# Batch-wide decays, a re-ordered start and half-column last stores in a linear-attention plus gated-MLP kernel

## Chip, cores and metric

One core of one Trainium2 chip. The metric is device time in microseconds (us) of one execution. Each execution has a state: "slow" ones lie over 1.5% above the fastest of the same kernel, and are left out of every comparison of times. A ratio below is the mean time of one kernel's fast runs over that of the other's of the same rounds, so it is not quite the ratio of the medians that are quoted beside it. The kernel before was timed again in each call, and the calls of the experiments ran on different chips of the same kind.

## The reference

Per batch (4) and head (8), blocks of 64 of 768 tokens; scores decay with the distance of tokens, a state carries what lies before the block. The result goes through a gated MLP whose gate is mixed over the tokens.

```python
Dmask = np.where(rel >= 0, lam ** rel, 0.0)
for b in range(nb):
    intra = (qb @ kb.T * Dmask) @ vb
    inter = (qb * lam ** (pos + 1)) @ kv_state
    out[b] = intra + inter
    kv_state = lam ** block * kv_state + (kb * lam ** (block - 1 - pos)).T @ vb
# x = heads side by side, (4, 768, 512)
h = relu(x @ w_in); u, v = halves of h
v_n = layernorm(v); v_s = w_spatial @ v_n + b_spatial      # over tokens
out = (u * v_s) @ w_out
```

## The kernel before

It works in 12 steps of 256 tokens, three to a batch. TensorE, GpSimd (POOL) and the sync engine (SP) run in the order of the program text; VectorE (DVE) and ScalarE (ACT) are ordered by the framework's scheduler. GpSimd prepares what was loaded (`ck` multiplies k by its decays into the tile `kd`, `cq` and `cv` cast q and v to bf16 as `qc` and `vc`), and in the same in-order queue issues the loads of the weights (`win`, `wsp`, `wout`). The load of v of step 1 is split: one half by SP, one by ScalarE.

```python
lam_bc = const.tile([P, H], FP32)
nc.scalar.dma_start(out=lam_bc, in_=lam...)
load_step(0)                               # k (two DMAs) and q on nc.sync; v too where n >= 2
load_v(0, nc.scalar, (0,))
load_step(1)
load_v(1, nc.sync, (1,))                   # cut: the tile is made here
for n in range(2, 4):
    load_step(n)
# ... cut ...
lq = const.tile([P, NG, T2], BF16)
for g in range(NG):
    last = nc.scalar.activation(out=lq[:, g, :], in_=qpos, func=AF.Exp, scale=logl[:, g:g + 1])
with tc.issue_after(last.ins):
    load_v(0, nc.scalar, (1,))
    load_v(1, nc.scalar, (0,))
# ... cut: kv_step ...
        sd = att.tile([P, NG, D], FP32, tag="sd", name=f"sd_{n}_{c}")
        nc.vector.tensor_tensor(out=sd, in0=prev, in1=lb, op=ALU.mult)
        nc.vector.tensor_tensor(out=s_sb[:, c], in0=sd, in1=pkv[:, c], op=ALU.add)
# ... cut: the order of the start (T: transposes, A: scores, K: states, O: outputs of attention) ...
run("""
    mask ck:0 cq:0 ck:1 cv:0 win:1 cq:1 cv:1 c:2 win:0 wsp wout c:3 lk:4 lk:5 lk:6
    T:0 K:0 A:0 T:1 O:0 K:1 A:1 pv:0:0 O:1 T:2 K:2 pv:0:1 A:2 pu:0:0 O:2
    c:4 pu:0:1 wt:0 pv:0:2 wt:2 pu:0:2 wt:4
    ...
""")
```

`wt:0` holds the first transposes of the spatial weight (tile `pwt`): nothing of batch 0 beyond them can run before that weight has landed. Its first matmul is the milestone in what follows.

Of the kernel before, what the change touches and what calls it, by code (L numbers as in the profile page):

```python
# [9 lines left out]
FP32 = mybir.dt.float32  # L10
BF16 = mybir.dt.bfloat16
I32 = mybir.dt.int32
# [6 lines left out]
def kernel(  # L19
# [13 lines left out]
    P = 128  # L33
# [57 lines left out]
    load_step(0)  # L91
    load_v(0, nc.scalar, (0,))
    load_step(1)
    st[1]["v_in"] = fin.tile([P, H, 2, D], FP32, tag="v_in", name="v_in_1")
    load_v(1, nc.sync, (1,))
    for n in range(2, 4):
        load_step(n)


    krev_i = const.tile([P, 1], I32)  # L100
    nc.gpsimd.iota(krev_i, pattern=[[0, 1]], base=P - 1, channel_multiplier=-1)

    qpos_i = const.tile([P, 2, 2, D], I32)
    nc.gpsimd.iota(qpos_i, pattern=[[1, 2], [0, 2], [2, D]], base=1, channel_multiplier=0)

# [4 lines left out]

    krev = const.tile([P, 1], FP32)
    nc.vector.tensor_copy(out=krev, in_=krev_i)
# [13 lines left out]
    for hh in range(2):  # L126
        rows = slice(hh * D, (hh + 1) * D)
        nc.vector.tensor_copy(out=logl[rows, :], in_=loglam[rows, hh::2])
    ldec = const.tile([P, H], FP32)
    nc.scalar.activation(out=ldec, in_=loglam, func=AF.Exp, scale=krev[:, 0:1])  # L130
    lm128 = const.tile([P, H], FP32)
    nc.scalar.activation(out=lm128, in_=loglam, func=AF.Exp, scale=-float(P))
    lq = const.tile([P, NG, T2], BF16)
    for g in range(NG):
        last = nc.scalar.activation(out=lq[:, g, :], in_=qpos, func=AF.Exp,
                                    scale=logl[:, g:g + 1])
    with tc.issue_after(last.ins):
        load_v(0, nc.scalar, (1,))
        load_v(1, nc.scalar, (0,))
    l128 = const.tile([P, NG], FP32)  # L140
    nc.scalar.activation(out=l128, in_=logl, func=AF.Exp, scale=float(P))
    sq_t = const.tile([P, 1], FP32)
    with tc.issue_after(last.ins):
        nc.scalar.activation(out=sq_t, in_=eps_t, func=AF.Sqrt)
    amask = const.tile([P, 2, 2, 2, P], FP32)

    def make_amask():
        for i in range(2):
            nc.vector.tensor_tensor(
                out=amask[:, i], in0=causal.unsqueeze(1).unsqueeze(1).broadcast_to((P, 2, 2, P)),  # L150
                in1=lm128[:, 4 * i:4 * i + 4].rearrange("p (g h) -> p h g", h=2).unsqueeze(3)
                .broadcast_to((P, 2, 2, P)), op=ALU.mult)

    win_sb = wpool.tile([P, NCH, DFF], BF16)
    wout_sb = wpool.tile([P, NCH, DM], BF16)
# [19 lines left out]
    def cast_step(n, parts=("k", "q", "v")):  # L175
        s = st[n]
        for part in parts:
            cast_part(s, n, part)

    def cast_part(s, n, part):  # L180
        if part == "k":
            kd = s["kd"] = att.tile([P, 2, H, D], BF16, tag="kd", bufs=4, name=f"kd_{n}")
            nc.gpsimd.tensor_tensor(out=kd.rearrange("p c h d -> p h c d"), in0=s["k_in"],  # L183
                                    in1=ldec.unsqueeze(2).unsqueeze(3).broadcast_to((P, H, 2, D)),
                                    op=ALU.mult)
        elif part == "q":
            qc = s["qc"] = att.tile([P, 2, H, D], BF16, tag="qc", bufs=4, name=f"qc_{n}")
            nc.gpsimd.tensor_copy(out=qc.rearrange("p m h d -> p h m d"), in_=s["q_in"])  # L188
        else:
            vc = s["vc"] = att.tile([P, H, 2, D], BF16, tag="vc", bufs=4, name=f"vc_{n}")  # L190
            nc.gpsimd.tensor_copy(out=vc, in_=s["v_in"])  # L191

    def trans_step(n):
        kd, qc = st[n]["kd"], st[n]["qc"]
        pt = two_banks([P, 2, NG, T2], f"pt_{n}", BF16)
        for j, src in ((0, kd), (1, qc)):
            for g in range(NG):
                for c in range(2):
# [4 lines left out]
        kT = att.tile([P, NG, T2], BF16, tag="kT", name=f"kT_{n}")  # L203
        nc.scalar.activation(out=kT, in_=pt[:, 0], func=AF.Copy)  # L204
        qT = att.tile([P, NG, 2, 2, D], BF16, tag="qT", name=f"qT_{n}")
        nc.vector.tensor_tensor(out=qT.rearrange("p g m a d -> p g (m a d)"), in0=pt[:, 1],  # L206
                                in1=lq, op=ALU.mult)
        st[n]["qT"], st[n]["kT"] = qT, kT
# [4 lines left out]
    def scores_step(n):  # L213
# [5 lines left out]
        for i in range(2):  # L219
            pam = two_banks([P, 2, 2, 2, P], f"pam_{n}_{i}")  # L220
            for g2 in range(2):
# [8 lines left out]
                in0=pam.rearrange("p h g c x -> p (h g) c x"),  # L230
                in1=amask[:, i].rearrange("p h g x -> p (h g) x").unsqueeze(2)
                .broadcast_to((P, 4, 2, P)), op=ALU.mult)

    def kv_step(n):
# [11 lines left out]
        s_sb = att.tile([P, 2, NG, D], BF16, tag="s_sb", name=f"s_{n}")  # L246
        lb = l128.unsqueeze(2).broadcast_to((P, NG, D))
        for c in range(nb):
            prev = s_sb[:, 0] if c == 1 else (st[n - 1]["s"][:, 1] if r > 0 else None)
            if prev is None:  # L250
                nc.vector.tensor_copy(out=s_sb[:, c], in_=pkv[:, c])
            else:
                sd = att.tile([P, NG, D], FP32, tag="sd", name=f"sd_{n}_{c}")
                nc.vector.tensor_tensor(out=sd, in0=prev, in1=lb, op=ALU.mult)  # L254
                nc.vector.tensor_tensor(out=s_sb[:, c], in0=sd, in1=pkv[:, c], op=ALU.add)
        st[n]["s"] = s_sb
# [81 lines left out]
    def pvs(b, f):  # L338
        m = gm[b]
        ps = two_banks([P, 2, 512], f"pvs_{b}_{f}")  # L340
        for i in range(2):
            cols = slice(i * HW_, (i + 1) * HW_)
            for s in range(NBLK):
# [7 lines left out]
                                op=ALU.mult)  # L351

    def po(b, r):
        gT = gm[b]["gT"]
        ps = two_banks([P, 2, DM], f"po_{b}_{r}")
# [5 lines left out]
        o_sb = ostg.tile([P, 2, DM], FP32, tag="o_sb", name=f"o_{b}_{r}")  # L361
        if (b, r) == (B - 1, NR - 1):
            dst = out[b, r * T2:(r + 1) * T2, :].rearrange("(j p) f -> p j f", p=P)
            half = slice(0, DM // 2), slice(DM // 2, DM)
            nc.scalar.activation(out=o_sb[:, 0], in_=ps[:, 0], func=AF.Copy)
            nc.sync.dma_start(out=dst[:, 0], in_=o_sb[:, 0])
            nc.vector.tensor_copy(out=o_sb[:, 1, half[0]], in_=ps[:, 1, half[0]])
            nc.scalar.activation(out=o_sb[:, 1, half[1]], in_=ps[:, 1, half[1]], func=AF.Copy)
            nc.sync.dma_start(out=dst[:, 1, half[0]], in_=o_sb[:, 1, half[0]])
            nc.scalar.dma_start(out=dst[:, 1, half[1]], in_=o_sb[:, 1, half[1]])  # L370
            return
        nc.scalar.activation(out=o_sb, in_=ps, func=AF.Copy)  # L372
# [3 lines left out]
    def wt_piece(s):  # L376
        ps = two_banks([P, 2, 1024], f"pwt_{s}", BF16)
        for j in range(2):
# [9 lines left out]
            "po": po, "wt": wt_piece, "win": load_win, "wsp": load_wsp, "wout": load_wout,  # L388
            "mask": make_amask, **{"c" + x: lambda n, x=x: cast_step(n, (x,)) for x in "kqv"}}

    def run(text):
# [5 lines left out]
    run("""  # L397
        mask ck:0 cq:0 ck:1 cv:0 win:1 cq:1 cv:1 c:2 win:0 wsp wout c:3 lk:4 lk:5 lk:6
        T:0 K:0 A:0 T:1 O:0 K:1 A:1 pv:0:0 O:1 T:2 K:2 pv:0:1 A:2 pu:0:0 O:2
        c:4 pu:0:1 wt:0 pv:0:2 wt:2 pu:0:2 wt:4  # L400
        c:5 lk:7 pvs:0:0 pvs:0:1 T:3 pvs:0:2 A:3 K:3 c:6 pvs:0:3 T:4 po:0:0
# [56 lines left out]
```

## Time and profile before

| | before |
|---|---|
| median, 4 runs | 177.33 us (176.49 to 177.79); the prediction had 3 of them, 177.02 |
| span of the profiled execution (a slow one) | 180.9 us |
| spatial weight issued, first `pwt` matmul | 28.39, 42.63 us |
| VectorE busy | 106.0 us |

The prediction below reads this profile stretch by stretch.

### The profile page before, as it was taken

To read this page: it belongs to the slowest core of one execution; us is meant where nothing else is said; L and a number is where in the kernel's file an instruction comes from. 1 tells how busy PE (TensorE), PEld (TensorE's weight loads), DVE (VectorE), ACT (ScalarE), POOL (GpSimd) and SP (SyncE) were. 2 spreads that over 40 slices of the span, in tenths; PEclk is the share of its full clock that TensorE was granted. 3 is DMA by queue.
4 is the path that set the end of the run, shared out by engine and by line. 5 is a ranking of instruction groups with operands and counts; after the bars stand their busy time and mean duration, and the time that the engine had idled before them with its cause. 6 is when DMAs were issued, how large, how long until landed. Compare 5 with 4: busy or idle time off the path is not lost.

```text
span 180.9 us, 3629 instructions
## 1 busy us (share of the span) xinstructions
PE 145.4 (80%) x1528; PEld 95.2 (53%) x1540; DVE 106.0 (59%) x182; ACT 77.3 (43%) x88; POOL 53.2 (29%) x50
## 2 busy tenths in 40 slices
PE   0041699399869999997955999999999999999890
PEld 0031566176636665676742655567866645776430
DVE  0712988921652889579998447179994713834400
ACT  2940057237911045677450014756822257660051
POOL 2439639400555566207556702000000000000000
PEclk9999999969987999999997899999999999999997
DMA  3999999999999999999899900630000026000036
GB/s 79 266 224 239 212 243 224 194 202 200 239 226 218 253 216 270 321 263 196 220 238 224 236 5 0 235 116 4 0 4 0 0 104 248 0 0 5 0 126 222
DMA packets 68497, 28.36 MB, mean 157 GB/s; under 512 B 50560, under 2 KB 65536, under 8 KB 68480
## 3 DMA queue, kind: packets, MB, share of 16 engines
q1 hardware_dynamic: 62560, 24.25, 58.2%
q0 software_dynamic: 2512, 2.95, 9.4%
q10 hardware_dynamic: 3408, 0.92, 2.7%
q8 instruction: 12, 0.20, 0.5%
q14 instruction: 5, 0.04, 0.1%
HBM read 24.78 MB, written 6.29 MB: 172 GB/s over the span
## 4 chain that ended last, share of the span: by engine, by line
PE 53%; DVE 17%; DMA 12%; SPq 9%; ACT 3%; issue 1%; POOL 1%; ACTq 0%; POOLq 0%
PE pvs L344 17%; PE po L359 10%; DMA wsp_raw<-in_moe_w_spatial_dram 8%; PE pv L313 8%; PE pu L334 7%; SPq L78 5%; DVE a L228 5%; DMA v_in<-in_v_dram 5%; DVE vn L325 4%; PE pvs L346 3%; PE pt L199 3%; DVE gT L348 2%; SPq L80 2%; DVE st L319 2%; SPq L69 2%; DVE sd L254 2%
## 5 line engine op out<-in xcount | busy, mean ns | idle before, releaser
L344 PE MATMUL pvs<-wt_sb,vn 128*128 128x384 bf16 x192 | 39.8, 343 | 5.2 <-DVE vn L325 5.1
L228 DVE TENSOR_TENSOR a<-pam,amask 128x1024 bf16<-128x1024 f32 x24 | 28.5, 1211 | 3.4 <-PE pam L225 3.4
L183 POOL TENSOR_TENSOR kd<-k_in,ldec 128x1024 bf16<-128x1024 f32 x12 | 23.0, 1917 | 23.2 <-DMA k_in<-in_k_dram 16.2
L344 PEld LDWEIGHTS <-vn 128*128 128x128 bf16 x192 | 19.4, 103 | 19.6 <-DVE vn L325 6.3
L204 ACT ACTIVATE kT<-pt 128x1024 bf16<-128x1024 bf16 x12 | 12.2, 1021 | 38.9 <-PE pt L199 38.9
L348 DVE TENSOR_TENSOR gT<-pvs,uT 128x768 bf16<-128x768 f32 x16 | 15.3, 957 | 19.6 <-PE pvs L346 19.6
L334 PE MATMUL pu<-xT,win_sb 128*128 128x256 bf16 x192 | 24.0, 284 | 2.9 <-DMA win_sb<-in_moe_w_in_dram 2.9
L313 PE MATMUL pv<-win_sb,xT 128*128 128x512 bf16 x89 | 22.0, 380 | 1.9 <-ACT xT L288 1.6
L359 PE MATMUL po<-wout_sb,gT 128*128 128x512 bf16 x91 | 21.7, 379 | 1.4 <-DVE a L228 0.7
L319 DVE BATCH_NORM_STATS2 st<-vh 128x6 f32<-128x512 bf16 x24 | 15.4, 682 | 12.5 <-ACT vh L316 12.3
L334 PEld LDWEIGHTS <-win_sb 128*128 128x128 bf16 x192 | 19.2, 102 | 6.6 <-DMA win_sb<-in_moe_w_in_dram 3.0
L288 ACT ACTIVATE xT<-pat 128x1024 bf16<-128x1024 f32 x12 | 15.8, 1320 | 15.6 <-PE pat L285 15.4
L191 POOL CAST vc<-v_in 128x1024 bf16<-128x1024 f32 x12 | 12.8, 1066 | 28.1 <-DMA v_in<-in_v_dram 20.9
L372 ACT ACTIVATE o<-po 128x1024 f32<-128x1024 f32 x11 | 11.3, 1025 | 18.3 <-PE po L359 18.3
L336 ACT ACTIVATE uT<-pu 128x1024 bf16<-128x1024 f32 x12 | 12.2, 1021 | 10.1 <-PE pu L334 10.1
L316 ACT ACTIVATE vh<-pv 128x1024 bf16<-128x1024 f32 x12 | 12.2, 1021 | 8.2 <-PE pv L313 8.1
L199 PE MATMUL pt<-ident,kd 128*128 128x128 bf16 x96 | 8.2, 234 | 9.1 <-POOL kd L183 9.1
L359 PEld LDWEIGHTS <-gT 128*128 128x128 bf16 x96 | 9.1, 98 | 11.7 <-DVE gT L348 1.3
L313 PEld LDWEIGHTS <-xT 128*128 128x128 bf16 x96 | 8.9, 98 | 11.3 <-ACT xT L288 2.0
L188 POOL CAST qc<-q_in 128x1024 bf16<-128x1024 f32 x12 | 12.9, 1076 | 5.9 <-DMA q_in<-in_q_dram 5.7
L206 DVE TENSOR_TENSOR qT<-pt,lq 128x1024 bf16<-128x1024 bf16 x12 | 8.2, 684 | 10.7 <-ACT kT L204 10.7
L325 DVE TENSOR_SCALAR vn<-vh,mv,rstd 128x512 bf16<-128x512 bf16 x24 | 14.1, 629 | 0.3
(54 smaller groups left out, 142.0 us busy)
## 6 DMA issues: line engine op xcount, KB each, us to landing
k_in<-in_k_dram SPq DMA_DIRECT2D x24, 256.0 KB, 5.3
q_in<-in_q_dram SPq DMA_DIRECT2D x12, 512.0 KB, 6.7
out_dram<-o SPq DMA_DIRECT2D x11, 512.0 KB, 3.1
v_in<-in_v_dram SPq DMA_DIRECT2D x21, 256.0 KB, 6.5
wsp_raw<-in_moe_w_spatial_dram POOLq DMA_DIRECT2D x1, 1152.0 KB, 14.2
win_sb<-in_moe_w_in_dram POOLq DMA_DIRECT2D x2, 512.0 KB, 8.2
v_in<-in_v_dram ACTq DMA_DIRECT2D x3, 256.0 KB, 6.3
wout_sb<-in_moe_w_out_dram POOLq DMA_DIRECT2D x1, 512.0 KB, 17.4
```

The costliest lines, as they stand in the source:

```text
L183: nc.gpsimd.tensor_tensor(out=kd.rearrange("p c h d -> p h c d"), in0=s["k_in"], in1=ldec.unsqueeze(2).unsqueeze(3).broadcast_to((P, H, 2, ...
L188: nc.gpsimd.tensor_copy(out=qc.rearrange("p m h d -> p h m d"), in_=s["q_in"])
L199: nc.tensor.transpose(out=pt[:, j, g, c * P:(c + 1) * P], in_=src[:, c, 2 * g:2 * g + 2, :].rearrange("p h d -> p (h d)"), identity=ident)
L228: nc.vector.tensor_tensor(out=a_sb[:, i].rearrange("p h g c x -> p (h g) c x"), in0=pam.rearrange("p h g c x -> p (h g) c x"), in1=amask[: ...
L288: nc.scalar.activation(out=xT[b][:, r].rearrange("p g (c d m) -> p (g c) m d", c=2, m=2), in_=po.rearrange("p g c (m d) -> p (g c) m d", m ...
L313: nc.tensor.matmul(out=ps[:, j], lhsT=x[:, r, c, j * P:(j + 1) * P], rhs=win_sb[:, c, DH:DFF], start=(c == 0), stop=(c == NCH - 1))
L319: nc.vector.bn_stats(out=m["st6"][:, t, :], in_=vh[:, t, :])
L325: nc.vector.tensor_scalar(out=m["vn"][:, t, :], in0=vh[:, t, :], scalar1=mv[:, t, 0:1], scalar2=rstd[:, t:t + 1], op0=ALU.subtract, op1=AL ...
L334: nc.tensor.matmul(out=ps[:, f], lhsT=win_sb[:, c, f * P:(f + 1) * P], rhs=x[:, r, c, :], start=(c == 0), stop=(c == NCH - 1))
L344: nc.tensor.matmul(out=ps[:, i, 0:HW_], lhsT=m["vn"][:, s, f * P:(f + 1) * P], rhs=wt_sb[:, s, cols], start=(s == 0), stop=False)
L348: nc.vector.tensor_tensor(out=m["gT"][:, f, :].rearrange("p (i x) -> p i x", i=2), in0=ps[:, :, 0:HW_], in1=m["uT"][:, f, :].rearrange("p ...
L359: nc.tensor.matmul(out=ps[:, j], lhsT=gT[:, c, t * P:(t + 1) * P], rhs=wout_sb[:, c, :], start=(c == 0), stop=(c == NCH - 1))
```

## The change

The intent: (1) count decays over a whole batch, so that states of blocks simply add and the product `sd` goes; (2) get the weights sooner; (3) store the last tile in pieces as they are done. The core of the diff, cut:

```diff
     load_step(0)
-    load_v(0, nc.scalar, (0,))
-    load_step(1)
-    load_v(1, nc.sync, (1,))
-    for n in range(2, 4):
+    load_v(0, nc.scalar)
+    for n in range(1, 4):
         load_step(n)
 # ... cut: ldec for six blocks, lq for three steps ...
     with tc.issue_after(last.ins):
-        load_v(0, nc.scalar, (1,))
-        load_v(1, nc.scalar, (0,))
+        load_v(1, nc.scalar)
+        for x in range(2, 4):
+            nc.scalar.activation(out=ldec[:, x, :], ...)
 # ... cut: tables(r) makes ldec and lq of r = 1, 2 on ScalarE, after kT of the step before ...
-                sd = att.tile([P, NG, D], FP32, tag="sd", name=f"sd_{n}_{c}")
-                nc.vector.tensor_tensor(out=sd, in0=prev, in1=lb, op=ALU.mult)
-                nc.vector.tensor_tensor(out=s_sb[:, c], in0=sd, in1=pkv[:, c], op=ALU.add)
+                nc.vector.tensor_tensor(out=s_sb[:, c], in0=prev, in1=pkv[:, c], op=ALU.add)
 # ... cut: po_last, three PSUM tiles and copies in place of one tile ...
-        mask ck:0 cq:0 ck:1 cv:0 win:1 cq:1 cv:1 c:2 win:0 wsp wout c:3 lk:4 lk:5 lk:6
-        T:0 K:0 A:0 T:1 O:0 K:1 A:1 pv:0:0 O:1 T:2 K:2 pv:0:1 A:2 pu:0:0 O:2
-        c:4 pu:0:1 wt:0 pv:0:2 wt:2 pu:0:2 wt:4
+        ck:0 cq:0 win:1 ck:1 cv:0 cq:1 cv:1 win:0 T:0 tab:1
+        ck:2 cq:2 wsp cv:2 c:3 wout lk:4 lk:5 lk:6
+        A:0 K:0 T:1 O:0 tab:2 A:1 K:1 pv:0:0 O:1 T:2 pv:0:1 A:2 K:2 pu:0:0 O:2 pu:0:1 wt:0 pv:0:2
+        c:4 wt:2 pu:0:2 wt:4
```

More of the change, by code (lines that the diff above doesn't have):

```diff
@@ L91 @@
     load_step(0)
-    load_v(0, nc.scalar, (0,))
-    load_step(1)
-    st[1]["v_in"] = fin.tile([P, H, 2, D], FP32, tag="v_in", name="v_in_1")
-    load_v(1, nc.sync, (1,))
-    for n in range(2, 4):
+    load_v(0, nc.scalar)
+    for n in range(1, 4):
         load_step(n)
-    krev_i = const.tile([P, 1], I32)
-    nc.gpsimd.iota(krev_i, pattern=[[0, 1]], base=P - 1, channel_multiplier=-1)
+    krev_i = const.tile([P, NBLK], I32)
+    nc.gpsimd.iota(krev_i, pattern=[[-P, NBLK]], base=P - 1, channel_multiplier=-1)
     qpos_i = const.tile([P, 2, 2, D], I32)
-    nc.gpsimd.iota(qpos_i, pattern=[[1, 2], [0, 2], [2, D]], base=1, channel_multiplier=0)
+    nc.gpsimd.iota(qpos_i, pattern=[[1, 2], [P, 2], [2, D]], base=1 - P, channel_multiplier=0)
     rel_i = const.tile([P, 2, D], I32)
@@ L109 @@
     make_identity(nc, ident)
-    krev = const.tile([P, 1], FP32)
+    krev = const.tile([P, NBLK], FP32)
     nc.vector.tensor_copy(out=krev, in_=krev_i)
@@ L128 @@
         nc.vector.tensor_copy(out=logl[rows, :], in_=loglam[rows, hh::2])
-    ldec = const.tile([P, H], FP32)
-    nc.scalar.activation(out=ldec, in_=loglam, func=AF.Exp, scale=krev[:, 0:1])
-    lm128 = const.tile([P, H], FP32)
-    nc.scalar.activation(out=lm128, in_=loglam, func=AF.Exp, scale=-float(P))
-    lq = const.tile([P, NG, T2], BF16)
+    lg_r = const.tile([P, NR - 1, NG], FP32)
+    for r in range(1, NR):
+        nc.vector.tensor_scalar(out=lg_r[:, r - 1, :], in0=logl, scalar1=float(r * T2), scalar2=None,
+                                op0=ALU.mult)
@@ L134 @@
+    ldec = const.tile([P, NBLK, H], FP32)
+    for c in range(2):
+        nc.scalar.activation(out=ldec[:, c, :], in_=loglam, func=AF.Exp, scale=krev[:, c:c + 1])
+    lq = const.tile([P, NR, NG, T2], BF16)
     for g in range(NG):
-        last = nc.scalar.activation(out=lq[:, g, :], in_=qpos, func=AF.Exp,
+        last = nc.scalar.activation(out=lq[:, 0, g, :], in_=qpos, func=AF.Exp,
                                     scale=logl[:, g:g + 1])
-    with tc.issue_after(last.ins):
-        load_v(0, nc.scalar, (1,))
-        load_v(1, nc.scalar, (0,))
@@ L140 @@
-    l128 = const.tile([P, NG], FP32)
-    nc.scalar.activation(out=l128, in_=logl, func=AF.Exp, scale=float(P))
     sq_t = const.tile([P, 1], FP32)
     with tc.issue_after(last.ins):
-        nc.scalar.activation(out=sq_t, in_=eps_t, func=AF.Sqrt)
-    amask = const.tile([P, 2, 2, 2, P], FP32)
-    def make_amask():
-        for i in range(2):
-            nc.vector.tensor_tensor(
-                out=amask[:, i], in0=causal.unsqueeze(1).unsqueeze(1).broadcast_to((P, 2, 2, P)),
-                in1=lm128[:, 4 * i:4 * i + 4].rearrange("p (g h) -> p h g", h=2).unsqueeze(3)
-                .broadcast_to((P, 2, 2, P)), op=ALU.mult)
+        load_v(1, nc.scalar)
@@ new lines, with tables @@
+        for x in range(2, 4):
+            nc.scalar.activation(out=ldec[:, x, :], in_=loglam, func=AF.Exp,
+                                 scale=krev[:, x:x + 1])
+    def tables(r):
+        with tc.issue_after(st[r - 1]["kT_ins"].ins):
+            if r == 1:
+                for x in range(4, NBLK):
+                    nc.scalar.activation(out=ldec[:, x, :], in_=loglam, func=AF.Exp,
+                                         scale=krev[:, x:x + 1])
+            for g in range(NG):
+                last = nc.scalar.activation(out=lq[:, r, g, :], in_=qpos, func=AF.Exp,
+                                            scale=logl[:, g:g + 1], bias=lg_r[:, r - 1, g:g + 1])
+        if r == NR - 1:
+            with tc.issue_after(last.ins):
+                nc.scalar.activation(out=sq_t, in_=eps_t, func=AF.Sqrt)
@@ L183, in cast_part @@
             nc.gpsimd.tensor_tensor(out=kd.rearrange("p c h d -> p h c d"), in0=s["k_in"],
-                                    in1=ldec.unsqueeze(2).unsqueeze(3).broadcast_to((P, H, 2, D)),
+                                    in1=ldec[:, 2 * (n % NR):2 * (n % NR) + 2, :]
+                                    .rearrange("p c h -> p h c").unsqueeze(3)
+                                    .broadcast_to((P, H, 2, D)),
                                     op=ALU.mult)
@@ L203, in trans_step @@
         kT = att.tile([P, NG, T2], BF16, tag="kT", name=f"kT_{n}")
-        nc.scalar.activation(out=kT, in_=pt[:, 0], func=AF.Copy)
+        st[n]["kT_ins"] = nc.scalar.activation(out=kT, in_=pt[:, 0], func=AF.Copy)
         qT = att.tile([P, NG, 2, 2, D], BF16, tag="qT", name=f"qT_{n}")
-        nc.vector.tensor_tensor(out=qT.rearrange("p g m a d -> p g (m a d)"), in0=pt[:, 1],
-                                in1=lq, op=ALU.mult)
+        st[n]["qT_ins"] = nc.vector.tensor_tensor(
+            out=qT.rearrange("p g m a d -> p g (m a d)"), in0=pt[:, 1], in1=lq[:, n % NR],
+            op=ALU.mult)
         st[n]["qT"], st[n]["kT"] = qT, kT
@@ L230, in scores_step @@
                 in0=pam.rearrange("p h g c x -> p (h g) c x"),
-                in1=amask[:, i].rearrange("p h g x -> p (h g) x").unsqueeze(2)
-                .broadcast_to((P, 4, 2, P)), op=ALU.mult)
+                in1=causal.unsqueeze(1).unsqueeze(1).broadcast_to((P, 4, 2, P)), op=ALU.mult)
     def kv_step(n):
@@ L246, in kv_step @@
         s_sb = att.tile([P, 2, NG, D], BF16, tag="s_sb", name=f"s_{n}")
-        lb = l128.unsqueeze(2).broadcast_to((P, NG, D))
-        for c in range(nb):
-            prev = s_sb[:, 0] if c == 1 else (st[n - 1]["s"][:, 1] if r > 0 else None)
-            if prev is None:
-                nc.vector.tensor_copy(out=s_sb[:, c], in_=pkv[:, c])
-            else:
-                sd = att.tile([P, NG, D], FP32, tag="sd", name=f"sd_{n}_{c}")
-                nc.vector.tensor_tensor(out=sd, in0=prev, in1=lb, op=ALU.mult)
-                nc.vector.tensor_tensor(out=s_sb[:, c], in0=sd, in1=pkv[:, c], op=ALU.add)
+        with tc.issue_after(st[n]["qT_ins"].ins):
+            for c in range(nb):
+                prev = s_sb[:, 0] if c == 1 else (st[n - 1]["s"][:, 1] if r > 0 else None)
+                if prev is None:
+                    nc.vector.tensor_copy(out=s_sb[:, c], in_=pkv[:, c])
+                else:
+                    nc.vector.tensor_tensor(out=s_sb[:, c], in0=prev, in1=pkv[:, c], op=ALU.add)
         st[n]["s"] = s_sb
@@ L351, in pvs, with po_last @@
                                 op=ALU.mult)
+    def po_last(b, r):
+        gT = gm[b]["gT"]
+        dst = out[b, r * T2:(r + 1) * T2, :].rearrange("(j p) f -> p j f", p=P)
+        o_sb = ostg.tile([P, 2, DM], FP32, tag="o_sb", name=f"o_{b}_{r}")
+        half = DM // 2
+        for i, (j, f0, fn, cp, eng) in enumerate((
+                (0, 0, DM, nc.scalar.copy, nc.sync),
+                (1, 0, half, nc.vector.tensor_copy, nc.sync),
+                (1, half, half, nc.scalar.copy, nc.scalar))):
+            ps = two_banks([P, 2, DM], f"po_{b}_{r}_{i}")[:, 0, 0:fn]
+            t = 2 * r + j
+            for c in range(NCH):
+                nc.tensor.matmul(out=ps, lhsT=gT[:, c, t * P:(t + 1) * P],
+                                 rhs=wout_sb[:, c, f0:f0 + fn], start=(c == 0),
+                                 stop=(c == NCH - 1))
+            cp(out=o_sb[:, j, f0:f0 + fn], in_=ps)
+            eng.dma_start(out=dst[:, j, f0:f0 + fn], in_=o_sb[:, j, f0:f0 + fn])
     def po(b, r):
+        if (b, r) == (B - 1, NR - 1):
+            return po_last(b, r)
         gT = gm[b]["gT"]
@@ L361, in po @@
         o_sb = ostg.tile([P, 2, DM], FP32, tag="o_sb", name=f"o_{b}_{r}")
-        if (b, r) == (B - 1, NR - 1):
-            dst = out[b, r * T2:(r + 1) * T2, :].rearrange("(j p) f -> p j f", p=P)
-            half = slice(0, DM // 2), slice(DM // 2, DM)
-            nc.scalar.activation(out=o_sb[:, 0], in_=ps[:, 0], func=AF.Copy)
-            nc.sync.dma_start(out=dst[:, 0], in_=o_sb[:, 0])
-            nc.vector.tensor_copy(out=o_sb[:, 1, half[0]], in_=ps[:, 1, half[0]])
-            nc.scalar.activation(out=o_sb[:, 1, half[1]], in_=ps[:, 1, half[1]], func=AF.Copy)
-            nc.sync.dma_start(out=dst[:, 1, half[0]], in_=o_sb[:, 1, half[0]])
-            nc.scalar.dma_start(out=dst[:, 1, half[1]], in_=o_sb[:, 1, half[1]])
-            return
         nc.scalar.activation(out=o_sb, in_=ps, func=AF.Copy)
@@ L388 @@
             "po": po, "wt": wt_piece, "win": load_win, "wsp": load_wsp, "wout": load_wout,
-            "mask": make_amask, **{"c" + x: lambda n, x=x: cast_step(n, (x,)) for x in "kqv"}}
+            "tab": tables, **{"c" + x: lambda n, x=x: cast_step(n, (x,)) for x in "kqv"}}
     def run(text):
```

## The prediction

> **What bounds the kernel now.** The profiled execution was a slow one (182.71 us, span 180.9) while the three timed runs have a median of 177.02, so I take differences from the trace and subtract them from 177.02. I began with the table of busy time by stretch (stretch, its length, busy time and instruction count of PE, PEld, DVE, ACT, POOL, then PE clock, DMA share, GB/s):
>
> ```profile
> 0.00:20.00 20.00, 2.84 (x36) 2.40 (x38) 7.18 (x13) 7.37 (x13) 10.75 (x17) 1.00 1.04 202
> 20.00:42.60 22.60, 18.79 (x238) 13.30 (x236) 16.88 (x29) 9.52 (x11) 9.28 (x9) 0.92 1.16 214
> 42.60:57.00 14.40, 12.05 (x88) 7.62 (x90) 5.75 (x8) 7.08 (x7) 6.92 (x5) 0.88 1.16 230
> 57.00:81.00 24.00, 23.42 (x291) 15.54 (x293) 18.39 (x28) 11.78 (x12) 10.20 (x8) 1.00 1.13 259
> 81.00:98.00 17.00, 11.71 (x183) 8.56 (x183) 15.92 (x26) 8.24 (x10) 10.83 (x8) 0.97 1.01 220
> 98.00:161.00 63.00, 62.03 (x623) 40.19 (x626) 37.63 (x75) 29.30 (x32) 5.23 (x4) 0.98 0.25 73
> 161.00:181.00 20.00, 14.53 (x81) 7.61 (x79) 4.26 (x5) 4.05 (x5) 0.00 (x0) 0.95 0.22 80
> ```
>
> TensorE is the bound from 57 to 81 and from 98 to 161: it is busy 85.5 of 87 us, and nothing taken from VectorE or ScalarE can pay there. It is short of work in three places: the first 57 us (33.7 busy of 57), 81 to 98 (11.7 of 17, with VectorE at 15.9), and the tail (5.5 idle of 20). A gain has to come from those. For the first I read the chain that ended last (start, length, what):
>
> ```profile
> 18.09 8.39 DMA v_in<-in_v_dram
> ...
> 27.65 0.74 POOL win_sb L162
> 28.39 14.19 DMA wsp_raw<-in_moe_w_spatial_dram
> ...
> 42.63 0.84 PE pwt L380 x12
> ```
>
> The start hangs on the spatial weight. GpSimd issues its load only at 28.39, because its program has the casts of step 2 and the load of half of w_in ahead of it; it lands at 42.58. GpSimd's timeline shows the order, and the cast that then starved:
>
> ```profile
> 24.14 1.04 POOL L188 CAST qc<-q_in 128x1024 bf16<-128x1024 f32 x1 [2.79 <-DMA q_in<-in_q_dram]
> 26.60 1.04 POOL L191 CAST vc<-v_in 128x1024 bf16<-128x1024 f32 x1 [1.42 <-DMA v_in<-in_v_dram]
> 27.59 0.80 POOL L162 DMA_DIRECT2D win_sb<-in_moe_w_in_dram  x1
> 28.39 0.83 POOL L166 DMA_DIRECT2D wsp_raw<-in_moe_w_spatial_dram  x1
> ...
> 45.35 1.04 POOL L191 CAST vc<-v_in 128x1024 bf16<-128x1024 f32 x1 [11.85 <-DMA v_in<-in_v_dram]
> ```
>
> For the second place, VectorE's timeline, and for the tail ScalarE's and VectorE's:
>
> ```profile
> 87.05 1.95 DVE L254 TENSOR_TENSOR sd<-s,l 128x256 f32<-128x256 bf16 x1
> ...
> 94.58 2.84 DVE L325 TENSOR_SCALAR vn<-vh,mv,rstd 128x512 bf16<-128x512 bf16 x2
> ```
>
> ```profile
> 176.07 0.60 ACT L365 ACTIVATE o<-po 128x512 f32<-128x512 f32 x1 [0.70 <-PE po L359]
> 176.70 0.42 DVE L367 COPY o<-po 128x256 f32<-128x256 f32 x1 [5.48 <-ACT o L365]
> 177.16 0.38 ACT L368 ACTIVATE o<-po 128x256 f32<-128x256 f32 x1 [0.49 <-DVE o L367]
> ```
>
> The last three copies run one after the other, and the first waited for all eight matmuls of the tile.
>
> **What the Trainium skill says.** "SBUF — State Buffer", Who interferes with whom: a VectorE instruction with two SBUF inputs contends with a GpSimd one that reads SBUF, under an exclusive lock; with one SBUF input it does not. The trace agrees: the 16 decay products sd (both inputs in SBUF) take 392 ns at least, 425 in the median and 1945 at most, and the long ones lie beside a GpSimd cast; the sums s (one input in PSUM) stay within 389 to 422. "DMA: Bandwidth & Descriptors", Queues, rings and completion order: each DMA engine takes the queues in turn, packet by packet. In the trace the weights' queue moved 2.43 MB between 26 and 48 us and the queue of the activations 2.05, and one v load took 17.4 us to land against a median of 6.5: earlier weights slow the activations. "TensorE: Matmul & The Clock Gate", Part 1: after an idle window of some 3.4 us the array runs at half clock. Here 16 matmuls of pu took 3.51 us right after a 2.87 us wait for w_in, and 1.92 at the next time. "ScalarE: Activation LUTs", What ACT_TABLE_LOAD costs: about 1283 ns for a load; the trace has three of 1.28 us.
>
> **The change part by part.**
>
> States just add. Sixteen sd products go: 16 x 737 ns mean = 11.8 us of VectorE, of which 16 x 0.42 = 6.7 is work and 5.1 is lock. The sum takes the old state straight from SBUF beside PSUM, so by the trace it stays at 0.41. Most lies under TensorE's bound. In 81 to 98 two of them, 1.95 and 0.42, stand before the statistics, the query product and the normalisation vn that pvs waits for. Putting the sums behind qT saves some delay of the score matmuls too. The lock may still catch vn (2.84 for two, against 0.73 free), since a kd of GpSimd runs at 94.34. I count 2.0 of the 2.4.
>
> The mask of 0 or 1 has the same shape: 24 products at 1.21 us stay. Building amask (2 x 1.5 = 3.0 us) goes, but VectorE then idled 7.2 us anyway: 0.
>
> More tables. ScalarE gets 8 more lq (8 x 0.49 = 3.9 us) and 5 more ldec (1.4), less 0.4 for two removed: some 4.9 us. ScalarE idled 10.13 us before the second kT, so the tables of r = 1 fit. Those of r = 2 with the square-root table load (4 x 0.49 + 1.28 + 0.2 = 3.4) come behind that kT and may hold the first xT. TensorE has a wait for the third q there anyway, so I charge 0.3.
>
> Order of loads. GpSimd's new order, timed with the old durations: kd:0 and qc:0 end at 10.5; w_in's second half is issued by 11.4 (before 15.96); kd:1 is bound by its load, 13.1 to 15.0; vc:0, qc:1 and vc:1 add 3.1, to 18.1; the other half of w_in is issued by 18.9 (before 27.59); kd:2 waits for its load at 19.5 and ends at 21.4; qc:2 waits for q as before and ends at 25.2; then the spatial weight, 3.2 us earlier than 28.39. Of its 14.2 us some 6.9 came after w_in's half had landed at 35.7. That half would now land at 18.9 + 8.2 = 27.1. So the spatial weight lands between 27.1 + 6.9 = 34.0 and 25.2 + 14.2 = 39.4; I take 36.5, 6 us earlier. TensorE must be ready as well: from 25.2 it has T, pv, A, K, pu, O, pu of step 2 (1.1 + 1.9 + 0.6 + 0.3 + 1.9 + 1.2 + 1.9 = 8.9 us) and some 2 us of waits for kT, qT and a, thus about 36. The new order also puts the spatial weight ahead of the cast of v of step 2, which could starve as v of step 3 did; I take 1 us off for that. Sum: 5.0. w_in will no longer be waited for at pu (2.87, and 1.6 of half clock), but that lies inside the same wait.
>
> After the weight the chain is unchanged, from 42.6 to 57: vn lost 2.4 to the lock (3.14 for two) and pvs ran some 2 us at half clock. Whether the shifted casts hit vn again is a coin toss; I count 0.5.
>
> The tail. Three tiles in place of one: the first copy starts while TensorE goes on, and after the last matmul there is one copy of 0.38, where before the last copy ended at 177.54 after matmuls ending near 176.0. 1.5 becomes 0.45; four more, narrower matmuls cost about 0.1. Gain 1.0.
>
> Sum: 5.0 + 2.0 + 0.5 + 1.0 - 0.3 = 8.2, thus 177.0 - 8.2 = **168.8 us**.
>
> **The rivals.** First, the wait for the spatial weight becomes a wait for v of step 2: the engines are full (share 1.04 to 1.16 all through the start), so the weights sooner are activations later. For it: the 17.4 us landing. Against: the weight alone is needed by everything of batch 0, and what is delayed behind it, steps 3 on, had 10 us to spare (the fourth kd was ready near 32 and its transposes ran at 57). If v lands 4 us late, the start gains 1 to 2: some 172. Second, the gain at the start arrives but is given back at 57 to 98, as the loads of steps 5 to 8 do not come sooner; GpSimd waits 16.2 us for k loads. For it: DMA stays at 1.0 or over until 100 us. Against: in 57 to 81 TensorE waited for none of them. That would make 171 to 173. Third, the start gets better than I count, as half clock and lock vanish at both places (2 + 2.4, and at 97 to 100 another 2): 164 to 165. Fourth, ScalarE's extra tables, with table loads back and forth if the scheduler mixes Exp and Sqrt, hold kT and xT: at 1.28 a load, 2 to 3 us lost, 171.
>
> **Range and chances.** The rivals spread from 164.5 to 173; the first two are likelier together than the third. Range 165.0 to 173.0. Faster by over 2% means below 173.5; only the first two rivals at once bring it there: 0.88, within 2% 0.10, slower 0.02.
>
> **What would show it.** The page after should have no sd line and VectorE 14 us or so less busy (11.8 + 3.0, less small pieces); the three w loads issued near 11, 19 and 25; the first pwt matmul at 35 to 39; pu no longer waiting for w_in; one copy after the last matmul. I am wrong in the start if the first pwt is at 40 or later, or if vc of step 2 waits over 4 us; wrong in the middle if pvs of the second batch still waits for vn over 2 us; wrong in the size if TensorE's idle time in 57 to 98, now some 6 us, grows.

## The result

187.78 us median of 4 runs (186.82 to 188.62), against 177.33 of 4: ratio 1.059, 95% interval 1.053 to 1.066. **Slower by 5.9%**, where 4.6% faster was predicted.

GpSimd's timeline of the changed kernel (start, length, engine, line, operation, operands, then in brackets the idle time before it and what ended it), against the one in the prediction:

```profile
15.82 1.03 POOL L194 CAST qc<-q_in 128x1024 bf16<-128x1024 f32 x1
29.57 1.04 POOL L197 CAST vc<-v_in 128x1024 bf16<-128x1024 f32 x1 [12.72 <-DMA v_in<-in_v_dram]
30.55 0.80 POOL L166 DMA_DIRECT2D win_sb<-in_moe_w_in_dram  x1
...
34.24 0.89 POOL L170 DMA_DIRECT2D wsp_raw<-in_moe_w_spatial_dram  x1
```

The cast of v of step 1 waits 12.7 us for its load, and both remaining weight loads stand behind it in the queue: half of w_in is issued at 30.6 (27.6 before), the spatial weight at 34.2 (28.4 before; 28.6 in a fast profile of the same start, that of the tail alone). The chain that ended last says the same in its own order:

```profile
22.68 6.76 DMA v_in<-in_v_dram
29.49 0.08 issue
29.57 1.05 POOL vc L197
30.66 0.64 PE pkv L249 x10
```

That load was issued only at 22.68, the other half at 19.99. ScalarE's timeline (ACTq is its sequencer):

```profile
18.41 1.02 ACT L210 ACTIVATE kT<-pt 128x1024 bf16<-128x1024 bf16 x1 [2.16 <-PE pt L205]
...
19.99 0.37 ACTq L69 DMA_DIRECT2D v_in<-in_v_dram  x1
...
22.55 1.28 ACT L157 ACT_TABLE_LOAD   x1
22.68 0.37 ACTq L69 DMA_DIRECT2D v_in<-in_v_dram  x1
```

Before, the two halves were issued at 7.55 (ScalarE) and 9.15 (SP). TensorE's timeline shows its own wait for the cast, and when `pwt` ran:

```profile
30.66 0.64 PE L249 MATMUL pkv<-vc,kd 128*64 128x64 bf16 x16 [9.63 <-POOL vc L197]
...
51.88 0.83 PE L395 MATMUL pwt<-ident,wsp_raw 128*128 128x128 bf16 x12
```

By which of the two did the late v reach `pwt`: through the late weight, or through TensorE's own wait? The weight, issued at 34.24, took 13.7 us to land, so it was there near 47.9, some 4 us before its first use at 51.88, and the trace has nobody waiting for it; nor did any instruction wait for w_in. What lay between is in the same chain, further on:

```profile
38.83 4.61 DVE vn L329 x2
43.45 1.13 DVE a L235
...
47.41 0.63 PE pat L282 x6
...
49.04 3.01 PE pu L338 x16
```

After the late start TensorE waited again, 2.52 us for the masked scores `a` and 2.14 for the state `s`, behind two normalisations vn that took 4.61 us, where two take 0.73 elsewhere in this trace. They ran beside GpSimd's qc, vc and kd (38.55 to 43.28), which followed one another without a break once v was there; that these slowed vn is likely and not isolated. So in this kernel TensorE's own late start and what came behind it set the time of `pwt`; the late weights would have done so only up to 47.9.

The table of busy time by stretch, over the first two stretches of before:

```profile
0.00:20.00 20.00, 7.13 (x88) 5.99 (x89) 5.52 (x15) 10.20 (x21) 9.02 (x15) 1.00 1.01 206
20.00:42.60 22.60, 11.25 (x134) 7.14 (x136) 9.39 (x13) 8.91 (x12) 12.99 (x12) 0.77 1.23 228
```

TensorE did more than before in the first 20 us (7.13 against 2.84: the scores of step 0 run at 14.69, not at 19.87), and then fell from 18.79 to 11.25 in the next 22.6, at a clock of 0.77. After the wait of 9.63 us, six matmuls of pv took 2.58 us, 0.43 each, where eight take 1.73 (0.22 each) later in the same trace.

So the first `pwt` matmul runs 9.3 us later (8.0 later than the 43.85 of the fast profile of the tail alone). The rest of the change is visible: VectorE is busy 94.6 us in place of 106.0 (11.4 less, where some 14 were expected), no `sd` line is left, one copy of 0.37 us follows the last matmul.

Why was that load late? Two candidates lay open. The compiled order of ScalarE's instructions has the two loads behind the tables of r = 2 and behind the square root, although the program text asks for them right after the tables of r = 0. And the same listing shows that each of them waits for a DMA semaphore (not the profile's output; the compiled program of the changed kernel, cut):

```
ScalarE  Activation sq_t
ScalarE  DMACopy v_in (step 1, first half)        waits DMAHW2
ScalarE  DMACopy v_in (step 1, second half)       waits DMAHW4
...
SP       DMACopy k_in (step 2, second half)       waits DMAHW2
...
SP       DMACopy v_in (step 2, first half)        waits DMAHW4
```

The framework hands eight semaphores, DMAHW0 to 7, in turn to the DMAs that ScalarE and SP issue. A load that takes a used one waits until its former user has landed. Here the loads of steps 2 and 3 stand ahead of v of step 1 in the program text, and have taken the turns ahead of it: its halves wait for the landing of k and of v **of step 2**. The trace's records of landings have those two at 19.78 and 22.66 us; the halves were issued at 19.99 and 22.68. For the second half the two agree within 0.02 us. The first half has a second explanation: in the compiled order xT stands ahead of it, and the matmuls that xT waits for ended at 19.94.

### The profile page after: what moved, and what is told of

It is laid out like the page before. It is cut to its first block, busy times and chain, and to the rows that moved or that the text cites. A ratio compares the mean times of both kernels' runs of the same rounds, so it can differ in the third digit from the quotient of the medians.

```text
span 185.9 us, 3633 instructions
## 1 busy us (share of the span) xinstructions
PE 145.5 (78%) x1532; PEld 96.3 (52%) x1544; DVE 94.6 (51%) x166; ACT 81.7 (44%) x99; POOL 53.0 (28%) x50
## 3 DMA queue, kind: packets, MB, share of 16 engines
q0 software_dynamic: 2512, 2.95, 9.2%
## 4 chain that ended last, share of the span: by engine, by line
PE 62%; DVE 13%; ACT 8%; DMA 8%; SPq 2%; POOL 2%; issue 2%; POOLq 0%; ACTq 0%
PE pvs L348 17%; PE pv L317 10%; PE pu L338 9%; PE po L384 9%; PE pt L205 4%; DMA k_in<-in_k_dram 4%; DVE a L235 4%; DMA v_in<-in_v_dram 4%; DVE vn L329 3%; PE pvs L350 3%; PE pat L289 3%; PE pat L282 2%; ACT kT L210 2%; ACT xT L292 2%; DVE st L323 2%; PE pam L232 2%
## 5 line engine op out<-in xcount | busy, mean ns | idle before, releaser
L348 PE MATMUL pvs<-wt_sb,vn 128*128 128x384 bf16 x192 | 38.4, 335 | 3.7 <-DVE vn L329 2.1
L235 DVE TENSOR_TENSOR a<-pam,causal 128x1024 bf16<-128x1024 f32 x24 | 28.5, 1212 | 4.7 <-PE pam L232 4.7
L187 POOL TENSOR_TENSOR kd<-k_in,ldec 128x1024 bf16<-128x1024 f32 x12 | 23.3, 1940 | 21.9 <-DMA k_in<-in_k_dram 16.2
L323 DVE BATCH_NORM_STATS2 st<-vh 128x6 f32<-128x512 bf16 x24 | 15.4, 682 | 19.4 <-ACT vh L320 19.2
L317 PE MATMUL pv<-win_sb,xT 128*128 128x512 bf16 x89 | 23.4, 397 | 2.1 <-ACT xT L292 1.6
L197 POOL CAST vc<-v_in 128x1024 bf16<-128x1024 f32 x12 | 12.5, 1042 | 34.2 <-DMA v_in<-in_v_dram 27.6
L384 PE MATMUL po<-wout_sb,gT 128*128 128x512 bf16 x83 | 20.0, 379 | 1.4 <-DVE a L235 0.7
L329 DVE TENSOR_SCALAR vn<-vh,mv,rstd 128x512 bf16<-128x512 bf16 x24 | 16.4, 725 | 0.3
L384 PEld LDWEIGHTS <-gT 128*128 128x128 bf16 x88 | 8.3, 97 | 10.8 <-DVE gT L352 1.3
## 6 DMA issues: line engine op xcount, KB each, us to landing
wsp_raw<-in_moe_w_spatial_dram POOLq DMA_DIRECT2D x1, 1152.0 KB, 13.7
```

Source lines behind the costliest of these rows:

```text
L187: nc.gpsimd.tensor_tensor(out=kd.rearrange("p c h d -> p h c d"), in0=s["k_in"], in1=ldec[:, 2 * (n % NR):2 * (n % NR) + 2, :] .rearrange( ...
L235: nc.vector.tensor_tensor(out=a_sb[:, i].rearrange("p h g c x -> p (h g) c x"), in0=pam.rearrange("p h g c x -> p (h g) c x"), in1=causal. ...
L317: nc.tensor.matmul(out=ps[:, j], lhsT=x[:, r, c, j * P:(j + 1) * P], rhs=win_sb[:, c, DH:DFF], start=(c == 0), stop=(c == NCH - 1))
L323: nc.vector.bn_stats(out=m["st6"][:, t, :], in_=vh[:, t, :])
L329: nc.vector.tensor_scalar(out=m["vn"][:, t, :], in0=vh[:, t, :], scalar1=mv[:, t, 0:1], scalar2=rstd[:, t:t + 1], op0=ALU.subtract, op1=AL ...
L348: nc.tensor.matmul(out=ps[:, i, 0:HW_], lhsT=m["vn"][:, s, f * P:(f + 1) * P], rhs=wt_sb[:, s, cols], start=(s == 0), stop=False)
```

## The experiments

Theory A: the late v of step 1 is the whole loss. Rival B: the new order of loads is slow in itself because the DMA engines are full. Rival C: ScalarE's added tables hold up the start. Theory A2, which came of the run "v of step 1 by ScalarE, in its place" below: the load is late because of the semaphores' turns, not because of its engine or its place in ScalarE's order.

### v of step 1 on the sync engine, ahead of step 2

```diff
-    for n in range(1, 4):
+    load_step(1)
+    load_v(1, nc.sync)
+    for n in range(2, 4):
         load_step(n)
...
-        load_v(1, nc.scalar)
```

> The changed kernel with one thing mended: both halves of v of step 1 are issued by the sync engine between the loads of steps 1 and 2, not by ScalarE, which issued them at 20.0 and 22.7 us. Theory A (the late v of step 1 blocks GpSimd's in-order queue, and with it the weights' loads): vc of step 1 runs by 20 us, the spatial weight is issued by 27 instead of 34.2, the first pwt matmul runs at 36 to 40 instead of 51.9, and the time is 167 to 173. Rival B (the new order of loads and weights is slow in itself, through full DMA engines): the wait moves to v or q of step 2, first pwt at 46 or later, the time 181 or more. Rival C (ScalarE's tables for r = 1 and 2 hold kT and xT): no weight wait, but xT and kT of step 1 late by 3 us or more, the time 175 to 181.

170.65 us median of 4 (170.00 to 173.49), before 178.82 of 11; ratio 0.956 (0.950 to 0.962). GpSimd's timeline:

```profile
20.37 1.04 POOL L198 CAST vc<-v_in 128x1024 bf16<-128x1024 f32 x1 [3.42 <-DMA v_in<-in_v_dram]
21.35 0.80 POOL L167 DMA_DIRECT2D win_sb<-in_moe_w_in_dram  x1
...
25.79 0.89 POOL L171 DMA_DIRECT2D wsp_raw<-in_moe_w_spatial_dram  x1
```

and TensorE's:

```profile
37.25 0.84 PE L396 MATMUL pwt<-ident,wsp_raw 128*128 128x128 bf16 x12 [1.30 <-DMA wsp_raw<-in_moe_w_spatial_dram]
```

Theory A's numbers; B and C fall. With this one load mended, the change is 4.4% faster than before: the load is worth 1.059 against 0.956, some 17 us. (The profile is of the slow one of the four runs; a fast one of the same start, in the last run below, has the first `pwt` at 37.82.) The edit changes the load's engine, its place and its semaphores' turns at once; later runs tell these apart.

### The kernel before with a late v of step 1

```diff
-    load_v(1, nc.sync, (1,))
-    for n in range(2, 4):
-        load_step(n)
+    load_step(2)
+    load_v(1, nc.sync)
+    load_step(3)
...
-        load_v(1, nc.scalar, (0,))
```

> The kernel before with one thing spoiled: both halves of v of step 1 are issued by the sync engine behind all loads of step 2, so at some 18 to 20 us. Nothing of the change is in it. Theory A: vc of step 1 waits until 26 to 28, the spatial weight is issued 5 to 9 us later than 28.39, and the time is 181 to 189. Rivals B and C: a late v costs little, since the loads of step 2 come sooner in exchange: 176 to 179.

184.01 us median of 4 (182.68 to 186.15); ratio 1.027 (1.019 to 1.035). GpSimd's timeline:

```profile
26.90 1.04 POOL L189 CAST vc<-v_in 128x1024 bf16<-128x1024 f32 x1 [9.17 <-DMA v_in<-in_v_dram]
...
32.71 0.83 POOL L164 DMA_DIRECT2D wsp_raw<-in_moe_w_spatial_dram  x1
```

The late load alone, without any of the change, delays the spatial weight by 4.3 us (4.1 against the fast profile of the tail alone; 5 to 9 was expected), the first `pwt` matmul to 47.43, and the end by 2.7%. Here v came 2.7 us sooner than in the changed kernel. And here, unlike there, the weights were waited for: TensorE stood 2.89 us for w_in and 0.83 for the spatial weight. So a late v does harm in the old kernel too, but 2.7% is far from the 17 us that the mended load is worth in the changed one; this run shows the direction, not the whole size.

### The arithmetic alone, the tail alone

The arithmetic, tables and mask of the change with loads, order and tail of before; and the kernel before with `po_last` only.

> The arithmetic of the change alone (decays over the whole batch, sums of states, mask of 0 or 1, ScalarE's tables), with the loads, the GpSimd order and the last stores of before. My sum gave 2.0 to 2.5 less 0.3 for it: 174 to 176. Rival C (ScalarE's tables hold up the start): 178 to 183.

177.15 us median of 4; ratio 0.994 (0.988 to 1.000): some 1.1 us, less than the 1.7 to 2.2 that were expected, and not clear of nothing. Rival C is not seen: the first `pwt` matmul runs at 44.56, against 43.85 in the run with the tail alone, whose start is that of before and whose profile, unlike that of before, is also of a fast run.

> The kernel before with the last stores of the change alone. My sum gave 1.0: ratio 0.993 to 0.996, and one copy of 0.38 us after the last matmul where there were three in a row. If the end is set by the landing of the stores and not by the copies: ratio 1.0.

178.41 us median of 6; ratio 0.998 (0.993 to 1.003): nothing shown. Yet the copies did become shorter, as expected. The share of busy time of the DMA engines and their GB/s, in 40 slices, suggests why. The kernel before, from 174 us on (a slice is 0.17 us):

```profile
DMA  0007999999810899999999999999930000000000
GB/s 0 0 0 257 398 374 386 398 410 398 328 47 0 328 410 386 398 386 386 374 386 363 386 386 340 334 351 310 369 100 0 0 0 0 0 0 0 0 0 0
```

The tail alone, from 168.5 on (0.21 us a slice):

```profile
DMA  0000000001999999506999999999999920000000
GB/s 0 0 0 0 0 0 0 0 0 70 350 400 360 420 370 380 210 0 260 410 360 400 370 380 410 360 380 405 310 350 325 340 60 0 0 0 0 0 0 0
```

In both, the second block of busy slices runs without a gap from the store of the tile before the last (512 KB) to the end. The new tail hands its three stores over sooner, into engines that are still busy.

### The new tail without the store before it

The 512 KB store of the tile before the last is left out. Its output is wrong, which doesn't matter for the time.

> Wrong on purpose: the kernel with the new tail alone, without the 512 KB store of the tile before the last. With the new tail alone the last three stores landed 2.8 to 3.2 us after issue, where they took 2.1 to 2.2 before, and the span ended 3.9 us after the last store was issued, where it was 3.0. If the DMA engines, still busy with the tile before, held them: they land 2.0 to 2.3 after issue, and the end comes 3.0 to 3.3 after the last issue. If not: 2.8 to 3.2 and 3.9 as before.

Time from issue to landing, first the tail alone, then without that store:

```profile
out_dram<-o SPq DMA_DIRECT2D x1, 256.0 KB, 3.0
out_dram<-o SPq DMA_DIRECT2D x1, 128.0 KB, 3.2
out_dram<-o ACTq DMA_DIRECT2D x1, 128.0 KB, 2.8
```

```profile
out_dram<-o SPq DMA_DIRECT2D x1, 256.0 KB, 2.1
out_dram<-o SPq DMA_DIRECT2D x1, 128.0 KB, 2.0
out_dram<-o ACTq DMA_DIRECT2D x1, 128.0 KB, 2.2
```

The span ends 3.2 us after the end of the last issue (171.46 to 174.7), where it was 3.9. So the store before held them, as far as one execution of unknown state can show; what the copies save is waited out there.

### The order alone

The kernel before with the new order of loads, GpSimd and TensorE, v of step 1 on the sync engine as mended above.

> The kernel before with the new order of loads, GpSimd and TensorE alone, v of step 1 on the sync engine as in the mended kernel; old arithmetic, old tail. The mended kernel gained 4.4% and the arithmetic alone 0.6%. If the parts add, the order alone gives ratio 0.96 to 0.97, first pwt at 36.5 to 39 instead of 42.6. If the order needs the arithmetic (qT held by the products of states, as at 17.3 us before), the ratio is 0.975 to 0.99 and A of step 0 runs at 17 us or later instead of 14.8.

172.67 us median of 4; ratio 0.969 (0.955 to 0.984), first `pwt` matmul at 38.73. A of step 0 runs at 14.77, so the order does not need the arithmetic. Most of the mended gain is here: 3.1% of 4.4; with 0.6 of the arithmetic and 0.2 of the tail it adds up to 3.9, within the intervals. (Only two of the four runs are fast ones, so the interval is wide.)

### v of step 1 by ScalarE, in its place

```diff
-        load_v(1, nc.scalar)
+        ld1 = load_v(1, nc.scalar)          # load_v now returns its last DMA
+    with tc.issue_after(ld1.ins):
         for x in range(2, 4):
             nc.scalar.activation(out=ldec[:, x, :], ...)
```

> The changed kernel with v of step 1 still issued by ScalarE, but in its order behind the tables of r = 1 instead of behind those of r = 2 (two ldec are made to follow it). A dose between: issued at some 14 to 16 us, where the changed kernel had 20.0 and 22.7 and the mended one 10.5 and 11.6. Theory A: vc of step 1 runs at 21 to 25 (mended 20.4, changed 29.6), the time is 171 to 176. If it were the engine or its queue that is slow, and not the moment of issue: 183 or more.

A miss: 183.25 us median of 4; ratio 1.025 (1.009 to 1.042), again from two fast runs of four. The compiled order had the loads behind the tables of r = 1, as meant. ScalarE's timeline:

```profile
14.14 2.06 ACT L155 ACTIVATE lq<-qpos,lg_r,logl 128x256 bf16<-128x256 f32 x4
19.75 3.47 ACTq L69 DMA_DIRECT2D v_in<-in_v_dram  x2
23.27 0.49 ACT L144 ACTIVATE ldec<-loglam,krev 128x8 f32<-128x8 f32 x2 [7.07 <-DMA v_in<-in_v_dram]
```

ScalarE had nothing left to do from 16.2 on, and still issued at 19.75. The order was mended and the load did not move. What it waited for is in the listing: semaphores DMAHW2 and DMAHW4 again, whose former users landed at 19.73 and 22.82 in this run. This made theory A2. (The two `ldec` stood behind the waiting loads here, and held the product kd of step 1 until 23.85; so the time is not a clean measure of a dose.)

### The weights ahead of the late v

```diff
-        ck:0 cq:0 win:1 ck:1 cv:0 cq:1 cv:1 win:0 T:0 tab:1
-        ck:2 cq:2 wsp cv:2 c:3 ...
+        ck:0 cq:0 win:1 ck:1 cv:0 cq:1 win:0 T:0 tab:1
+        ck:2 cq:2 wsp cv:1 cv:2 c:3 ...
```

> The changed kernel, its late v of step 1 left as it is, but in GpSimd's order the cast of that v goes behind the weights' loads and the k and q of step 2, so that only TensorE waits for it. If most of the loss came through GpSimd's queue (weights issued late): the spatial weight is issued by 27, first pwt at 42 to 46 instead of 51.9, time 176 to 181. If it came through TensorE's own wait for that v, or the weights now starve it: first pwt at 49 or later, time 185 or more.

188.95 us median of 4; ratio 1.067 (1.051 to 1.084). The spatial weight is issued at 25.26, as early as it should be, and the kernel is no faster. ScalarE's timeline, then GpSimd's:

```profile
20.47 0.38 ACTq L69 DMA_DIRECT2D v_in<-in_v_dram  x1
...
27.34 0.37 ACTq L69 DMA_DIRECT2D v_in<-in_v_dram  x1
```

```profile
25.26 0.89 POOL L170 DMA_DIRECT2D wsp_raw<-in_moe_w_spatial_dram  x1
...
39.14 2.03 POOL L197 CAST vc<-v_in 128x1024 bf16<-128x1024 f32 x2 [12.44 <-DMA v_in<-in_v_dram]
```

The weights now slow v of step 2, on whose landing the second half of v of step 1 waits: it is issued at 27.34 instead of 22.68, and TensorE waits 19.4 us for the cast; the first `pwt` runs at 55.97. So it is not enough to say that GpSimd's queue passed the delay on to the weights; the late v stops TensorE by itself.

### One loop moved

The changed kernel; only the making of the loads of steps 2 and 3 stands below that of v of step 1 in the program text. SP's own order of loads is the same.

```diff
     load_v(0, nc.scalar)
-    for n in range(1, 4):
-        load_step(n)
+    load_step(1)
...
         load_v(1, nc.scalar)                 # after the tables of r = 0, as in the change
         for x in range(2, 4): ...            # ldec, as in the change
+    for n in range(2, 4):
+        load_step(n)
```

> The changed kernel with nothing but one loop moved: the program text makes the loads of steps 2 and 3 after the load of v of step 1, so that this load takes an earlier turn of the eight DMA semaphores. It is still ScalarE that issues it, after the same table; the sync engine's loads keep their order. Theory A2 (v of step 1 was issued late because it had to wait for the semaphores of k and v of step 2, which landed at 19.8 and 22.7): it is issued by ScalarE at 7.5 to 11, vc of step 1 runs at 17 to 21, the spatial weight is issued by 27, first pwt at 36 to 39, time 167 to 172. If the turn of the semaphores had no part in it: issued at 14 or later, time 176 or more.

173.38 us median of 6 (171.32 to 174.74, three of them slow); ratio 0.966 (0.960 to 0.973). In the compiled order the loads now stand right behind the tables of r = 0, and wait for DMAHW1 and DMAHW3, whose former users are loads of step 0 (landed at 5.31 and 6.81). ScalarE's timeline, then GpSimd's:

```profile
7.24 0.38 ACTq L69 DMA_DIRECT2D v_in<-in_v_dram  x1
...
7.65 0.59 ACTq L69 DMA_DIRECT2D v_in<-in_v_dram  x1
```

```profile
19.47 1.03 POOL L198 CAST vc<-v_in 128x1024 bf16<-128x1024 f32 x1
...
24.93 0.89 POOL L171 DMA_DIRECT2D wsp_raw<-in_moe_w_spatial_dram  x1
```

Same engine, same text around it, same weights' order: moving one loop is worth 1.059 against 0.966. The engine is not the cause, since ScalarE can issue early, and the semaphores' turns alone hold the load, since "v of step 1 by ScalarE, in its place" mended the place and did not move it (19.75, after a landing at 19.73). In this run the compiled place moved forward together with the turns; mended turns with the late place were not tried, so what the place would cost by itself stays open. It is a little behind the load on SP. There v of step 1 starts later (10.48) and does not meet k of step 1 on its way: that k lands at 15.46 here, and its product kd waits 2.95 us for it (0.35 with the load on SP).

### The last batch's first two tiles in halves

The kernel of the last run, with the outputs of the last batch's first two tiles copied and stored in two halves each; then the same with the load on SP.

> The same, with the outputs of the last batch's first two tiles copied and stored in halves as soon as each half is ready. If the end is held by the DMA engines, which were busy without a break from the store of the tile before the last on, the 512 KB before the last starts 0.5 to 0.9 us sooner and the end comes 0.4 to 0.9 us sooner: 0.3 to 0.5% less than the kernel of this call without it. If not, the two are alike, or it is slower by the copies.

172.97 us median of 7, four of them slow; ratio 0.955 (0.947 to 0.962) beside 0.966 of the kernel without it. The intervals overlap.

> The best of both: the changed kernel with v of step 1 on the sync engine between the loads of steps 1 and 2 (ratio 0.956 alone) and the last batch's first two tiles stored in halves (0.9664 to 0.9549 in the call before, with ScalarE's load). If the two add: ratio 0.944 to 0.952, time 167.5 to 170. If the last run's difference was noise: 0.953 to 0.960.

170.02 us median of 6 (168.83 to 171.40); ratio 0.958 (0.952 to 0.964), beside 0.956 for the load on SP without it. It was run at another time. So no gain is shown for the halves, and the difference of the run before is not to be built on. (One execution of before took 292 us and counts as slow.) The lowest ratio of the versions without halves is that of v of step 1 on the sync engine, 0.956; the intervals of that and of ScalarE's early load, 0.966, touch.

## Why the prediction was wrong

**The step that failed** is in "Order of loads": "vc:0, qc:1 and vc:1 add 3.1, to 18.1". It took for granted that v of step 1 lands as before. The cast ran at 29.57, not by 18.1, TensorE stood 9.63 us for it, and everything after it in that paragraph slid: half of w_in issued at 30.55 instead of 18.9, the spatial weight at 34.24 instead of 25.2, the first `pwt` at 51.9 instead of 36.5. The diff shows the cause: the load changes engine and place, and its new place is behind the loads of two later steps, of which it shares DMA semaphores with k and v of step 2. The prediction put the two conditions of `pwt` close together, the weight landed at 36.5 and TensorE ready at about 36; in the changed kernel they were met near 47.9 and at 51.88, so TensorE's own path was the later one. I timed the new order "with the old durations" and never asked when this load would be issued. I did not know of the semaphores' turns, but the question would have been due without them.

**The rivals.** The first had the right shape (a wait for a v takes the place of the one for the weight) and the wrong load and cause: v of step 2, through full DMA engines. The fourth expected ScalarE's queue to cost, through tables and kT; the queue did cost, but through a load that was held in it. None reached beyond 173.

**The other terms, measured once the load is mended.** Start: predicted 5.0 and 0.5 for what follows it; the order alone gives 3.1% or 5.4 us (interval 2.8 to 8.0). Its inner times held within 2.5 us: half of w_in 18.9 predicted, 21.35 measured; the spatial weight 25.2 and 25.79; `pwt` 36.5 and 37.25. Arithmetic: predicted 2.0 less 0.3 for the tables; measured 1.1 (0 to 2.2). In the mended kernel, as at 94.58 before, two vn of the second batch took over 2 us together, beside a kd of GpSimd (85.73 to 87.81); the prediction's name for it, the lock, is not isolated by any run. VectorE's timeline

```profile
85.63 2.34 DVE L330 TENSOR_SCALAR vn<-vh,mv,rstd 128x512 bf16<-128x512 bf16 x2
```

against 0.73 free. In the fast profile of the tail alone none of the vn from 66 to 98 us is slow (0.72 to 0.74 for two), so it does not always happen. Tail: predicted 1.0; 0.4 measured, with zero inside its interval, for a reason that I had not looked at: I followed the copies and not the stores. Sum of the mended kernel: predicted 8.2, measured 4.4% of 177, or 7.8. The size of the sum held and the sign of the result did not, for one load; that the sum came so near is partly luck, since the arithmetic and the tail brought less than predicted (the three parts measured alone add up to 6.9).

**Two readings of the trace that were wrong.** The prediction says that the long sd lie beside a GpSimd cast. Of the five long ones, those at 20.17, 69.81 and 87.05 began beside a product kd, and only two beside a cast. And it lays half clock to an idle window of some 3.4 us, where its own case was idle for 2.87 us only; in the run with the late v in before, the same 16 matmuls after a wait of 2.89 us took 1.92 us, at full clock. So the half clock that it counted on losing does not follow from the length of that wait alone.

**What stays open.** The mended kernel with SP and that with ScalarE's load differ by 1%; the 2.95 us wait fits it, but no run isolates it. They were run at other times. Between a fast profile of the changed kernel (span 185.9) and one of the best order (168.0, the run with halves on SP) 14.1 of the 17.9 us lie ahead of the first `pwt`; where the other 3.8 go was not tested.

## What to carry to other kernels

When a change moves a load, work out when it will be issued: which engine's queue it stands in, what is ahead of it there, and which earlier loads it waits for, since a framework that shares a few DMA semaphores makes a load wait for the landing of loads that merely stand ahead of it in the program text. An in-order queue that mixes casts and weight loads turns one late input into late weights, but look whether anyone waits for them: in the changed kernel nobody did, and putting the weights first did not help, because TensorE itself stood waiting for the late input. At the end of a kernel follow the stores and not the copies: here earlier copies showed no gain, with the DMA engines still busy with the store before.

## What the Trainium skill lacked or had wrong

- "DMA: Bandwidth & Descriptors", Why a DMA increments its semaphore by 16 and not by 1, asks for one semaphore for each DMA in flight. It does not say what a framework does that has few of them: the compiled program makes a load wait at its issuing engine until the former user of its semaphore has landed. Here the late v was issued at 19.99 and 22.68 us, after landings at 19.78 and 22.66, and at 7.24 and 7.65 with another turn.
- The same page, Issuing engines are not separate DMA queues, says that several issuing engines only save the sequencer's issue time. That passage leaves out the wait of a DMA for a semaphore, which the page elsewhere places on the issuing engine: ScalarE's next activation stood 7.07 us behind a held load.
- The same page, Specifications, gives a limit of some 358 GB/s to HBM for a core, without saying there that this is a core's part when two stream; its section Bandwidth says it. The stores at the end ran at 374 to 410 in most full slices of 0.17 us, in a program on one core.
- "ScalarE: Activation LUTs", What ACT_TABLE_LOAD costs: the load of 1283 ns is confirmed, but of the further drain of about 1380 ns none is seen: in the kernel before a load of 1.28 us starts at 8.44, as the activation ahead of it ends (7.94 + 0.49), and the next activation starts at 9.73.
- "TensorE: Matmul & The Clock Gate", Part 1, puts the half clock after at least one idle window of some 3.4 us. After 9.63 us of idle time six matmuls took 0.43 us each instead of 0.22, which agrees; but in the kernel before 16 matmuls took 3.51 us after an idle time of 2.87, and in the run with the late v in before 1.92 after 2.89. The length of the gap just before them does not tell the two apart.
